# Decay attention in float32: both heads' score matmuls in one PSUM pair, and V products side by side

## The chip, the core and the metric

The kernel runs on one core of one Trainium2 chip. The metric is device time in microseconds (us) from the program's start to its end; lower is better. The engines are TensorE (PE, with its weight loads as PEld), VectorE (DVE), ScalarE (ACT), GpSimd (POOL) and the DMA queues, which SP, ACT and POOL issue to.

## The reference

Three stages follow each other on 2304 tokens (4 batches of 576) of width 512 (8 heads of 64), all in float32. The change touches the first one alone.

```python
scores = scale * q @ k.T                          # per batch and head, 576 x 576
decay = cum[:, None] - cum[None, :]               # cum: running sum of log(clip(f))
scores = where(causal, -1e9, scores + decay)
attn = exp(scores - max(scores)); attn /= sum(attn) + 1e-9
x = (attn @ v)                                    # heads side by side: 2304 x 512
h = x @ w_in; g = h * tanh(softplus(h)); y = g @ w_out
out = max(y @ w1, y @ w2, y @ w3) @ w_out2
```

## The kernel before, in words

**Attention.** A job is one batch and one pair of heads: 4 x 4 = 16 jobs. q and k of both heads are transposed on PE (`prep`, L290) so that head 0 has its 64 dimensions on partitions 0 to 63 (`U`) and head 1 on 64 to 127 (`L`). A job has two units: g = 0 for query rows 0 to 255 and g = 1 for rows 256 to 575. `scores` (L326) makes, per unit, one tile of 128 query rows per head and row block `qt` with (qt + 1) x 128 key columns (128 and 256 columns in g = 0, 384 and 512 in g = 1), and in g = 1 also one tile that holds the last 64 query rows of both heads, as two chunks of 288 columns (`h is None`). For each tile `score_mm` (L318) issues one float32 matmul (two PE rows in the profile) into a PSUM bank `sc`. DVE adds the decay, takes the row's extreme and writes the tile P to SBUF in one operation (L366); ACT makes the exponential with its row sum (L372), DVE the reciprocal (L344, L345), POOL scales P (`scale_rows`).

`av` (L384) comes two units later (`LEAD`): PE turns P in blocks of 128 x 128 into a PSUM bank `pp` (L394), DVE and ACT in turn copy the bank to SBUF (`TA`, `TB`), and the V products (L403) multiply them with v. A product's output has 64 partitions: head 0's are the upper half of the bank `av`, head 1's the lower half. `SEQA`, `SEQB`, `PRODA` and `PRODB` say in which order the blocks are turned and which product reads which columns: in g = 1 a block row `kt` has five blocks, head 0's two, the mixed one, head 1's two, and a head's product reads 320 neighbouring columns. ACT then copies the accumulator to `xt` (L411) in two or four pieces, and SP stores it to `x_d`.

**PSUM** has eight banks: four for `sc`, `tr` and `pp` together (tag `ps`), two for `av`, two for `h`.

**h.** `h_steps` computes h = x @ w_in, 24 matmuls (mm3, L184 to L186) a step of 256 tokens and 256 columns, 72 steps. It needs x of a whole block of 256 tokens, so its first steps come after the first batch's four jobs. `w_in` comes in by DMA and is converted on ACT, DVE and POOL in pieces during the first units. Attention is emitted with high priority and the scheduler fills PE's queue with `h` matmuls between; the order in each engine's queue is fixed when the program is built. When attention is done, its buffers go to `w_out`, and the rest of `h`, then y and the last stage follow.

Of the kernel before, what the change touches and what calls it, by code (L numbers as in the profile page):

```python
# [9 lines left out]
F32 = mybir.dt.float32  # L10
# [3 lines left out]
AF = mybir.ActivationFunctionType  # L14
ALU = mybir.AluOpType
PSUM = bass.MemoryType.PSUM
# [16 lines left out]
BLK = 256  # L33
BLK2 = 512
LEAD = 2

TBW = 2432
SEQA = [(0, 0, 0), (0, 0, 1), (0, 1, 0), (0, 1, 1), (1, 0, 1), (1, 1, 1)]  # L40
ATA = [128 * i for i in range(6)]
PRODA = [(0, 0, 0, 0, 256, False, 4), (0, 1, 256, 0, 256, False, 4),
         (1, 0, 512, 128, 128, True, 6), (1, 1, 640, 128, 128, True, 6)]
SEQB = [(kt, h, qt) for kt in range(3) for h, qt in ((0, 2), (0, 3), (0, 4), (1, 3), (1, 2))]
SEQB += [(3, 0, 3), (3, 0, 4), (3, 1, 3), (4, 0, 4)]
ATB = [128 * i for i in range(19)]
PRODB = [(kt, h, 640 * kt + 320 * h, 0, 320, False, 5 * kt + (3, 5)[h]) for kt in range(3) for h in range(2)]
PRODB += [(3, 0, 1920, 128, 192, False, 19), (3, 1, 2112, 0, 192, False, 19),
          (4, 0, 2304, 256, 64, True, 19), (4, 1, 2368, 0, 64, True, 19)]


def turned_layout(seq, banks, at, products):

    out, n = [], 0
    for size in banks:
        blocks = [(*b, c) for b, c in zip(seq[n:n + size], at[n:n + size])]
        n += size
        ready = [p for p in products if p[6] <= n and p[6] > n - size]
        out.append((blocks, [p[:6] for p in ready]))
    return out  # L60


LAYA = turned_layout(SEQA, (4, 2), ATA, PRODA)
LAYB = turned_layout(SEQB, (4, 4, 4, 3, 4), ATB, PRODB)


@with_exitstack
def tile_decay_attention__mish_ff__max3_ff(
# [148 lines left out]
    ap_ = at.enter_context(tc.tile_pool(name="ap", bufs=1, side="right"))  # L217
    as_ = at.enter_context(tc.tile_pool(name="as", bufs=1, side="right"))
    aw = at.enter_context(tc.tile_pool(name="aw", bufs=1, side="right"))
    hps = sa.enter_context(tc.tile_pool(name="hps", bufs=2, space=PSUM))  # L220
    aps = at.enter_context(tc.tile_pool(name="aps", bufs=1, space=PSUM, side="right"))

    def att_psum(name):
        return aps.tile([128, 512], F32, name=name, tag="ps", bufs=4)

    U, L = slice(0, 64), slice(64, 128)

# [4 lines left out]


    TA = aw.tile([128, 768], F32, name="TA")
    TB = aw.tile([128, TBW], F32, name="TB")
    for t in sums:
        nc.vector.memset(t, 1.0)
    q4 = [as_.tile([128, 128], F32, name=f"q4_{i}") for i in range(2)]
# [1 line left out]
        nc.gpsimd.memset(t, 0.0)  # L240
    for t in vs:
        nc.gpsimd.memset(t[U, 512:640], 0.0)
    count = dict(unit=0, bank=0)

    def load(i, b, hp):

# [71 lines left out]
    def score_mm(J, h, qt, dst, c0, w):  # L318
        if h is None:
            lhs, rows = J["q4"], slice(0, 128)  # L320
        else:
            rows = (U, L)[h]
            lhs = J["q"][rows, qt * 128:qt * 128 + 128]
        nc.tensor.matmul(dst, lhs, J["k"][rows, c0:c0 + w], start=True, stop=True, skip_group_check=True)  # L324

    def scores(J, g):  # L326


        P = {}
        u = count["unit"]  # L330
        count["unit"] += 1
        sm = sums[u % 4]
        mn = aw.tile([128, 6], F32, name="mn", bufs=4)
        rr = aw.tile([128, 5], F32, name="rr", bufs=4)
        tiles = [(None, 4)] if g == 1 else []
        tiles += [(h, qt) for qt in ((0, 1) if g == 0 else (2, 3)) for h in range(2)]
        made = []
        col = 0

        def scale_rows(part):  # L340

            cs = slice(part[0], part[-1] + 1)
            with tc.high_priority(400):
                nc.vector.tensor_scalar(rr[:, cs], sm[:, cs], 1e-9, None, op0=ALU.add)  # L344
                nc.vector.reciprocal(rr[:, cs], rr[:, cs])  # L345
                for ci in part:
                    nc.gpsimd.tensor_scalar(made[ci], made[ci], rr[:, ci:ci + 1], 1.0, op0=ALU.mult, op1=ALU.mult)  # L347

        for ci, (h, qt) in enumerate(tiles):
            wd = (qt + 1) * 128 if qt < 4 else S  # L350
            Pt = aw.tile([128, wd], F32, name=f"P{qt}_{h}", bufs=LEAD)
            made.append(Pt)
            if h is None:
                P[4] = Pt
            else:
                P[h, qt] = Pt
            cb = decay(J, h, qt)
            if h is None:
                cb = [cb[:, n:n + 1] for n in range(2)]
            else:  # L360
                cb = [cb]
            for pi, (c0, w) in enumerate([(0, wd)] if qt < 4 else [(0, 288), (288, 288)]):
                sc = att_psum("sc")
                score_mm(J, h, qt, sc[:, :w], c0, w)
                like = lambda t: t.rearrange("p (a c) -> p a c", a=cb[pi].shape[1])
                nc.vector.tensor_tensor_reduce(  # L366
                    out=like(Pt[:, c0:c0 + w]), in0=like(sc[:, :w]), in1=cb[pi],
                    scale=-scale, scalar=(3e38 if pi == 0 else mn[:, col - 1:col]),
                    op0=ALU.add, op1=ALU.min, accum_out=mn[:, col:col + 1],
                )  # L370
                col += 1
            nc.scalar.activation(  # L372
                Pt, Pt, AF.Exp, scale=-1.0, bias=mn[:, col - 1:col], accum_out=sm[:, ci:ci + 1],
            )
            if ci == 2 - (g == 0):
                scale_rows(list(range(ci + 1)))
        scale_rows(list(range(3 - (g == 0), len(tiles))))
        return P

    def av(J, g, P):  # L380


        q0 = 0 if g == 0 else 256
        gw = 256 if g == 0 else 320  # L384
        T = (TA, TB)[g]
        xt = aw.tile([128, gw], F32, name=f"xt{g}")
        acc = aps.tile([128, 512], F32, name="av", bufs=2)
        for blocks, products in (LAYA, LAYB)[g]:
            pp = att_psum("pp")
            for n, (kt, h, qt, c) in enumerate(blocks):  # L390

                k0 = kt * 128 if kt < 4 else S - 128
                Pt = P[4] if qt == 4 else P[h, qt]
                nc.tensor.transpose(pp[:, n * 128:n * 128 + 128], Pt[:, k0:k0 + 128], ident)  # L394
            w, c = len(blocks) * 128, blocks[0][3]
            count["bank"] += 1
            if count["bank"] % 2:
                nc.vector.tensor_copy(T[:, c:c + w], pp[:, :w])
            else:
                nc.scalar.activation(T[:, c:c + w], pp[:, :w], AF.Copy)  # L400
            for kt, h, c, off, w, last in products:
                n = 4 * h + kt if kt < 4 else 8 + h
                nc.tensor.matmul(  # L403
                    acc[(U, L)[h], off:off + w], J["vs"][:, n * 64:n * 64 + 64], T[:, c:c + w],
                    start=kt == 0, stop=last, skip_group_check=True,
                )
        parts = [(0, 0, 0, gw)]
        parts += [(1, 0, 256, 64), (1, 64, 128, 128), (1, 192, 0, 128)] if g else [(1, 0, 0, 256)]
        for h, c, o, w in parts:
            rows = (U, L)[h]  # L410
            nc.scalar.activation(xt[rows, o:o + w], acc[rows, c:c + w], AF.Copy)  # L411
        t0 = J["b"] * S + q0
        done = 0
        while done < gw:
            blk, off = divmod(t0 + done, BLK)
            n = min(gw - done, BLK - off)
            pace[:] = [nc.sync.dma_start(x_d[blk][:, J["hp"], off:off + n], xt[:, done:done + n])]
            done += n

    def attention():  # L420


        jobs = [(b, hp) for b in range(B) for hp in range(H // 2)]
        J = {0: load(0, *jobs[0])}
        yield 0
        prep(J[0])
        J[1] = load(1, *jobs[1])
        tok = 0
        units = [(ji, g) for ji in range(len(jobs)) for g in range(2)]
        pend = []  # L430
        for n in range(len(units) + LEAD):
            if n < len(units):
                ji, g = units[n]
                pend.append((J[ji], g, scores(J[ji], g)))
            if n >= LEAD:
                unit = pend.pop(0)
                av(*unit)
                if unit[0]["hp"] == H // 2 - 1:
                    tok = unit[0]["b"] * S + (256, S)[unit[1]]
            if n < len(units):  # L440
                if g == (ji == 0) and ji + 1 < len(jobs):
                    prep(J[ji + 1])
                if g == 1 and ji + 2 < len(jobs):
                    J[ji + 2] = load(ji + 2, *jobs[ji + 2])
            yield tok


    done = 0

    def ready(i):  # L450
        return BLK * (i + 1) <= done

    def h_steps():
# [9 lines left out]
        for n, (i, fp) in enumerate(order):  # L463
# [6 lines left out]
            while fp not in loaded:  # L470
                next(wgen, None)
            xh, xl = xs[i]
            h = hps.tile([128, 2, BLK], F32, name="h")
            for a in range(2):
                fs = slice(a * 128, (a + 1) * 128)
                for c in range(KD):
# [404 lines left out]
```

## Time and profile before

| what | value |
|---|---|
| median of 3 runs | 963.77 us (963.77 to 964.42) |
| the profiled execution | 962.3 us |
| its span | 960.5 us, 15156 instructions |
| PE busy | 936.5 us (97%) |
| DVE, ACT, POOL busy | 506.6, 417.6, 229.1 us |
| score matmuls (L324) and V products (L403) in PE's rows | 320 and 448 |

Busy time is what an engine's instructions cover; matmuls are pipelined and their ends are modelled, so the start of the next matmul tells more than a row's length. The last V product starts at 352.5 us and the last `h` matmul at 488.8 us.

### The profile page before, as it was taken

Reading aid. Unit: us, or ns where it says so; the run is one execution under the profiler, and the core shown is the slowest. Engines: PE = TensorE matmul, PEld = TensorE weight load, DVE = VectorE, ACT = ScalarE, POOL = GpSimd, SP = SyncE. Lnnn points to the kernel's source line nnn. Section 1 sums busy time; section 2 is a strip of 40 time slices with the busy share of each in tenths; the row PEclk is TensorE's granted clock in tenths of the full one; section 3 lists DMA queues with packets and bytes.
Section 4 is the critical chain, followed back from the end, with each engine's and each line's share of the span. In section 5 each row is a group of like instructions: output and inputs, shape, how many; then the busy total and the mean of one; then the engine's idle time right before and its main releaser. Section 6 shows DMA issues by size and latency. Waiting matters only on the chain.

```text
span 960.5 us, 15156 instructions
## 1 busy us (share of the span) xinstructions
PE 936.5 (97%) x5312; PEld 755.2 (79%) x5312; DVE 506.6 (53%) x1164; ACT 417.6 (43%) x967; POOL 229.1 (24%) x319
## 2 busy tenths in 40 slices
PE   5998999999999999999999999999999999999998
PEld 3554666777777679999988878789888999889986
DVE  4558688533344428970026657567694345614440
ACT  5778666545454444232236445455343222412221
POOL 3456654344223210111002000000021133103310
PEclk9999999999999999999999999999999999999999
DMA  7776656644443139752245666666388544334401
GB/s 165 170 205 192 208 173 191 181 111 130 117 142 102 35 93 332 244 185 78 99 148 184 193 216 201 215 219 197 114 289 332 175 132 132 104 98 124 115 32 71
DMA packets 143931, 154.77 MB, mean 161 GB/s; under 512 B 68656, under 2 KB 103984, under 8 KB 143856
## 3 DMA queue, kind: packets, MB, share of 16 engines
q1 hardware_dynamic: 121328, 114.48, 40.3%
q10 hardware_dynamic: 19840, 25.17, 7.5%
q0 software_dynamic: 2688, 14.16, 4.0%
q8 instruction: 42, 0.69, 0.3%
q14 instruction: 33, 0.27, 0.1%
HBM read 107.55 MB, written 46.21 MB: 160 GB/s over the span
## 4 chain that ended last, share of the span: by engine, by line
PE 75%; DMA 12%; ACT 5%; DVE 4%; issue 3%; SPq 1%; POOL 0%; ACTq 0%; POOLq 0%; DVEq 0%
DMA g<-h_d 9%; PE sc L324 8%; PE h L184 7%; PE h L186 7%; PE h L185 7%; PE av L403 7%; PE q L185 5%; PE q L184 5%; PE q L186 5%; PE pp L394 4%; PE o L184 2%; PE o L185 2%; PE o L186 2%; PE y L184 2%; PE y L186 2%
## 5 line engine op out<-in xcount | busy, mean ns | idle before, releaser
L184 PE MATMUL h<-xh,wi 128*128 128x256 f32 x576 | 167.6, 291 | 0.5 <-ACT he L486 0.5
L185 PE MATMUL h<-xl,wi 128*128 128x256 f32 x576 | 166.8, 290 | 0.0
L186 PE MATMUL h<-xh,wi 128*128 128x256 f32 x576 | 166.5, 289 | 0.0
L184 PEld LDWEIGHTS h<-xh,wi 128*128 128x128 f32 x576 | 109.7, 190 | 12.7 <-issue 10.0
L615 DVE TENSOR_TENSOR gl<-g,gh 128x512 fp32r<-128x512 f32 x72 | 51.0, 709 | 129.4 <-ACT gh L614 127.1
L185 PE MATMUL y<-gl,wo 128*128 128x512 f32 (+1 forms) x320 | 118.2, 369 | 0.0
L186 PE MATMUL y<-gh,wo 128*128 128x512 f32 (+1 forms) x320 | 117.3, 369 | 0.0
L186 PEld LDWEIGHTS h<-xh,wi 128*128 128x128 f32 x576 | 109.8, 191 | 9.0 <-issue 8.6
L185 PEld LDWEIGHTS h<-xl,wi 128*128 128x128 f32 x576 | 109.7, 191 | 8.9 <-issue 6.5
L184 PE MATMUL y<-gh,wo 128*128 128x512 f32 (+1 forms) x320 | 109.2, 371 | 1.6 <-ACT ze L643 1.1
L372 ACT ACTIVATE P<-P,mn 128x128 f32<-128x128 f32 (+3 forms) x128 | 71.4, 558 | 75.0 <-DVE mn L366 70.9
L608 ACT ACTIVATE g<-g 128x512 f32<-128x512 f32 x72 | 45.4, 631 | 90.6 <-DMA g<-h_d 89.5
L347 POOL TENSOR_SCALAR P<-P,rr 128x128 f32<-128x128 f32 (+3 forms) x128 | 70.6, 565 | 58.4 <-DVE rr L345 38.6
L324 PE MATMUL sc<-kT,qT 64*128 64x128 f32 (+3 forms) x256 | 78.6, 503 | 3.4 <-ACT qT L301 3.0
L184 PEld LDWEIGHTS y<-gh,wo 128*128 128x128 f32 x320 | 60.1, 189 | 13.0 <-ACT ze L643 1.8
L185 PEld LDWEIGHTS y<-gl,wo 128*128 128x128 f32 x320 | 60.3, 189 | 10.4 <-DVE gl L615 0.7
L186 PEld LDWEIGHTS y<-gh,wo 128*128 128x128 f32 x320 | 60.3, 189 | 9.7
L403 PE MATMUL av<-TB,vs 128*64 128x320 f32 (+2 forms) x320 | 60.9, 394 | 0.1
L394 PE MATMUL pp<-ident,P 128*128 128x128 f32 x320 | 56.7, 284 | 0.5 <-DVE mn L366 0.5
L807 DVE TENSOR_TENSOR u<-q,p 128x448 f32<-128x448 f32 x36 | 22.4, 622 | 62.6 <-PE q L186 62.5
L324 PEld LDWEIGHTS sc<-kT,qT 64*128 64x128 f32 x256 | 31.8, 197 | 29.0 <-issue 10.3
L486 ACT ACTIVATE he<-h 128x512 f32<-128x512 f32 x46 | 27.3, 594 | 58.1 <-PE h L186 55.6
(141 smaller groups left out, 1897.9 us busy)
## 6 DMA issues: line engine op xcount, KB each, us to landing
g<-h_d SPq DMA_DIRECT2D x72, 256.0 KB, 3.4
s<-s_d SPq DMA_DIRECT2D x72, 256.0 KB, 2.9
h_d<-he ACTq DMA_DIRECT2D x46, 256.0 KB, 2.5
wr<-in_moe_w_out_dram SPq DMA_DIRECT2D x22, 512.0 KB, 4.1
wr<-in_moe_w_dram SPq DMA_DIRECT2D x24, 384.0 KB, 4.2
s_d<-sk POOLq DMA_DIRECT2D x12, 768.0 KB, 5.1
cb<-cum_d SPq DMA_DIRECT2D x32, 256.0 KB, 4.0
wr<-in_moe_w_in_dram SPq DMA_DIRECT2D x32, 256.0 KB, 4.1
```

Source lines behind the costliest of these rows:

```text
L184: nc.tensor.matmul(ps, wh, xh, start=start, stop=False, skip_group_check=True)
L185: nc.tensor.matmul(ps, wh, xl, start=False, stop=False, skip_group_check=True)
L186: return nc.tensor.matmul(ps, wl, xh, start=False, stop=stop, skip_group_check=True)
L324: nc.tensor.matmul(dst, lhs, J["k"][rows, c0:c0 + w], start=True, stop=True, skip_group_check=True)
L347: nc.gpsimd.tensor_scalar(made[ci], made[ci], rr[:, ci:ci + 1], 1.0, op0=ALU.mult, op1=ALU.mult)
L372: nc.scalar.activation(Pt, Pt, AF.Exp, scale=-1.0, bias=mn[:, col - 1:col], accum_out=sm[:, ci:ci + 1],)
L394: nc.tensor.transpose(pp[:, n * 128:n * 128 + 128], Pt[:, k0:k0 + 128], ident)
L403: nc.tensor.matmul(acc[(U, L)[h], off:off + w], J["vs"][:, n * 64:n * 64 + 64], T[:, c:c + w], start=kt == 0, stop=last, skip_group_check= ...
L486: nc.scalar.activation(he, h, AF.Copy)
L608: nc.scalar.activation(g, g, AF.Mish)
L615: on_dve[:] = [nc.vector.tensor_tensor(out=gl, in0=g, in1=gh, op=ALU.subtract)]
L807: add = lambda eng, o, x, y: eng.tensor_tensor(out=o, in0=x, in1=y, op=ALU.add)
```

## The change

Scores: when head 0's tile comes up, one PSUM tile of two banks is taken and both heads' matmuls are issued into it one after the other; DVE then reads the halves in turn. The mixed tile of g = 1 comes last instead of first and puts its two chunks into the two banks. V products: each bank of turned blocks holds both heads' blocks of one `kt`, a product is 256, 128 or 64 columns wide, and both heads' products stand next to each other; the mixed block's 64 columns per head are products of their own. The accumulator has the same column order for both heads, so one copy moves it to `xt`. PSUM: three banks for `tr` and `pp`, a pair `sc` (two banks), one for `av`, and two that hold a second pair until the eighth unit and then `h`.

```diff
+def turned_layout(g):
+    if g == 0:
+        runs = [[(0, 0, 256)], [(1, 128, 128)]]
+        banks = [[(0, h, qt) for h in range(2) for qt in range(2)], [(1, h, 1) for h in range(2)]]
+    else:
+        runs = [[(kt, 0, 256)] for kt in range(3)] + [[(3, 128, 128), (0, 256, 64), (1, 256, 64)]]
+        runs += [[(2, 256, 64), (3, 256, 64), (4, 256, 64)]]
+        banks = [[(kt, h, qt) for h in range(2) for qt in (2, 3)] for kt in range(3)]
+        banks += [[(3, 0, 3), (3, 1, 3), (0, None, 4), (1, None, 4)], [(kt, None, 4) for kt in (2, 3, 4)]]
...
-    hps = sa.enter_context(tc.tile_pool(name="hps", bufs=2, space=PSUM))
+    early = ExitStack()
+    eps = [early.enter_context(tc.tile_pool(name="eps", bufs=1, space=PSUM, reuse_waits="tile"))]
     aps = at.enter_context(tc.tile_pool(name="aps", bufs=1, space=PSUM, side="right"))
     def att_psum(name):
-        return aps.tile([128, 512], F32, name=name, tag="ps", bufs=4)
+        return aps.tile([128, 512], F32, name=name, tag="ps", bufs=3)
...
-        tiles = [(None, 4)] if g == 1 else []
-        tiles += [(h, qt) for qt in ((0, 1) if g == 0 else (2, 3)) for h in range(2)]
+        tiles = [(h, qt) for qt in ((0, 1) if g == 0 else (2, 3)) for h in range(2)]
+        if g == 1:
+            tiles.append((None, 4))
...
+            if not h:
+                count["sc"] += 1
+                pair = (aps if count["sc"] % 2 or not eps else eps[0]).tile([128, 2, 512], F32, name="sc", bufs=1)
+                for n in range(2):
+                    if h is None:
+                        score_mm(J, h, qt, pair[:, n, :288], 288 * n, 288)
+                    else:
+                        score_mm(J, n, qt, pair[:, n, :wd], 0, wd)
             for pi, (c0, w) in enumerate([(0, wd)] if qt < 4 else [(0, 288), (288, 288)]):
-                sc = att_psum("sc")
-                score_mm(J, h, qt, sc[:, :w], c0, w)
+                sc = pair[:, h or pi]
...
-        acc = aps.tile([128, 512], F32, name="av", bufs=2)
+        acc = aps.tile([128, 512], F32, name="av", bufs=1)
...
+            for kt, off, w, *at in products:
+                for h in range(2):
+                    n = 4 * h + kt if kt < 4 else 8 + h
+                    nc.tensor.matmul(
+                        acc[(U, L)[h], off:off + w], J["vs"][:, n * 64:n * 64 + 64], T[:, at[h]:at[h] + w],
+                        start=kt == 0 and off == 0, stop=kt == (1 if g == 0 else 4), skip_group_check=True,
+                    )
+        nc.scalar.activation(xt, acc[:, :gw], AF.Copy)
...
+            if n == 6 + LEAD:
+                eps.clear()
+                early.close()
+                eps_h.append(sa.enter_context(tc.tile_pool(name="hps", bufs=2, space=PSUM, reuse_waits="tile")))
```

The scheduler puts PE's queue together anew. Before, in a g = 1 unit of the middle of attention (`av` are V products, `pp` turned blocks, `sc` scores; an `x2` is two equal neighbours):

```order
L403 MATMUL av<-TB,vs_186 64x320
L394 MATMUL pp<-ident,P_0_2225 128x128
L403 MATMUL av<-TB,vs_186 64x320 x2
L394 MATMUL pp<-ident,P_None 128x128
L394 MATMUL pp<-ident,P_1_2230 128x128
L394 MATMUL pp<-ident,P_None 128x128
L324 MATMUL sc<-kT,qT 128x128
L403 MATMUL av<-TB,vs_186 64x320
L324 MATMUL sc<-kT,qT 128x128
```

The two 128-column scores, one per head, have a V product between them, and the first V product stands alone. The same kind of place now, at the end of a g = 1 unit:

```order
L410 MATMUL av<-TB,vs_187 64x128 x2
L410 MATMUL av<-TB,vs_187 64x64 x4
L400 MATMUL pp<-ident,P_0_2726 128x128
L400 MATMUL pp<-ident,P_1_2732 128x128
L183 MATMUL h<-xh,wi_161 128x256
L322 MATMUL sc<-kT,qT 128x512 x2
L410 MATMUL av<-TB,vs_187 64x64 x6
```

Both heads' scores are neighbours, V products stand in twos, and the mixed blocks' 64-column products follow in fours and sixes. In SP's queue the first fetch of `w_in` before, behind the stores of five units of x (`x_d`):

```order
L250 DMA rawq_181<-in_q_dram 128x4x64
L254 DMA rawq_181<-in_q_dram 64x64
L152 DMA wr<-in_moe_w_in_dram 128x512 x4
L307 DMA vs_187<-in_v_dram 128x4x64 x2
L311 DMA vs_187<-in_v_dram 64x2x64
L417 DMA x_d_61<-xt_1022 128x256
```

and now, behind the stores of three:

```order
L252 DMA rawq_183<-in_q_dram 64x64
L149 DMA wr<-in_moe_w_in_dram 128x512 x4
L259 DMA cb<-cum_d 128x2x256 x2
L248 DMA rawk_182<-in_k_dram 128x4x64 x2
L305 DMA vs_186<-in_v_dram 128x4x64 x2
```

The fetch has moved two units forward.

## Rows read from the trace of the kernel before

**Rows 1.** The page, first part: busy time, share of the span, instructions.

```profile
PE 936.5 (97%) x5312; PEld 755.2 (79%) x5312; DVE 506.6 (53%) x1164; ACT 417.6 (43%) x967; POOL 229.1 (24%) x319
```

**Rows 2.** Busy time by stretch; columns as in the first line.

```profile
core 0: us, PE busy (x) PEld busy (x) DVE busy (x) ACT busy (x) POOL busy (x), PEclk, DMA share, GB/s
0.00:110.00 110.00, 93.58 (x519) 55.37 (x520) 66.86 (x229) 74.63 (x226) 59.73 (x109) 0.95 0.71 186
110.00:353.00 243.00, 243.00 (x1550) 171.19 (x1549) 121.36 (x365) 128.72 (x357) 92.08 (x139) 1.00 0.44 129
353.00:489.00 136.00, 135.53 (x1065) 132.17 (x1064) 64.61 (x115) 42.25 (x73) 14.17 (x8) 1.00 0.53 182
```

**Rows 3.** Waits of PE from 120 to 420 us: total, times, longest.

```profile
PE h L184 <- ACT he L486: 0.5, 1, 0.5
```

**Rows 4.** Timeline of PE near 175 us: start, length, engine, line, shapes.

```profile
174.46 0.49 PE L324 MATMUL sc<-kT,qT 64*128 64x128 f32 x2
174.88 0.75 PE L403 MATMUL av<-TB,vs 128*64 128x320 f32 x2
175.56 0.48 PE L324 MATMUL sc<-kT,qT 64*128 64x128 f32 x2
175.98 0.39 PE L185 MATMUL h<-xl,wi 128*128 128x256 f32 x1
176.20 0.28 PE L186 MATMUL h<-xh,wi 128*128 128x256 f32 x1
176.32 0.27 PE L184 MATMUL h<-xh,wi 128*128 128x256 f32 x1
...
176.75 0.76 PE L403 MATMUL av<-TB,vs 128*64 128x320 f32 x4
177.44 0.70 PE L324 MATMUL sc<-kT,qT 64*128 64x256 f32 x2
```

**Rows 5.** Timeline of PE at four other places: a stretch and the next row.

```profile
191.77 1.12 PE L324 MATMUL sc<-kT,qT 64*128 64x512 f32 x2
192.82 0.38 PE L185 MATMUL h<-xl,wi 128*128 128x256 f32 x1
...
216.23 1.13 PE L324 MATMUL sc<-kT,qT 64*128 64x512 f32 x4
217.28 0.38 PE L184 MATMUL h<-xh,wi 128*128 128x256 f32 x1
...
272.73 0.49 PE L324 MATMUL sc<-kT,qT 64*128 64x128 f32 x4
273.15 0.39 PE L185 MATMUL h<-xl,wi 128*128 128x256 f32 x1
...
179.92 0.66 PE L403 MATMUL av<-TB,vs 128*64 128x192 f32 x8
180.51 0.70 PE L324 MATMUL sc<-kT,qT 64*128 64x256 f32 x2
```

**Rows 6.** Busy time by stretch, three slices of 24 us.

```profile
72.00:96.00 24.00, 20.08 (x109) 11.20 (x108) 20.42 (x59) 19.79 (x54) 16.69 (x20) 0.99 0.68 193
120.00:144.00 24.00, 24.00 (x143) 15.48 (x141) 19.80 (x48) 16.01 (x43) 13.26 (x17) 1.00 0.59 173
192.00:216.00 24.00, 24.00 (x157) 17.50 (x157) 9.37 (x33) 11.24 (x34) 9.90 (x15) 1.00 0.42 111
```

**Rows 7.** Groups by line and shape, 110 to 353 us: busy, mean ns, idle before.

```profile
L398 DVE COPY TB<-pp 128x512 f32<-128x512 f32 x21 | 14.5, 689 | 17.1 <-PE pp L394 17.0
L366 DVE CUSTOM_DVE_ANT_1 P<-sc,cb 128x512 f32<-128x512 f32 x20 | 13.7, 686 | 3.7 <-PE sc L324 3.6
L169 DVE SCALAR_TENSOR_TENSOR wt<-wr,wt 128x512 int32<-128x512 int32 x11 | 10.6, 964 | 0.1
L411 ACT ACTIVATE xt<-av 64x320 f32<-64x320 f32 x11 | 4.7, 429 | 7.9 <-PE av L403 7.9
```

**Rows 8.** Loads: V products from 110 to 353 us, and `h` of the whole span.

```profile
L403 PEld LDWEIGHTS av<-TB,vs 128*64 128x64 f32 x220 | 14.7, 135 | 10.5 <-issue 4.6
L184 PEld LDWEIGHTS h<-xh,wi 128*128 128x128 f32 x576 | 109.7, 190 | 12.7 <-issue 10.0
```

More of the change, by code (lines that the diff above doesn't have):

```diff
@@ L35 @@
 LEAD = 2
[L39 to L59, printed above, removed]
-    return out
-LAYA = turned_layout(SEQA, (4, 2), ATA, PRODA)
-LAYB = turned_layout(SEQB, (4, 4, 4, 3, 4), ATB, PRODB)
+def turned_layout(g):
[7 more added lines that the diff above has]
+        banks += [[(3, 0, 3), (3, 1, 3), (0, None, 4), (1, None, 4)], [(kt, None, 4) for kt in (2, 3, 4)]]
+    out, c = [], 0
+    for blocks, bank in zip(banks, runs):
+        products, at = [], c
+        for kt, off, w in bank:
+            products.append((kt, off, w, at, at + w))
+            at += 2 * w
+        out.append((c, blocks, products))
+        c += len(blocks) * 128
+    return out
+LAYOUT = [turned_layout(g) for g in range(2)]
 @with_exitstack
@@ L234, in tile_decay_attention__mish_ff__max3_ff @@
     TA = aw.tile([128, 768], F32, name="TA")
-    TB = aw.tile([128, TBW], F32, name="TB")
+    TB = aw.tile([128, 2432], F32, name="TB")
     for t in sums:
@@ L242, in tile_decay_attention__mish_ff__max3_ff @@
         nc.gpsimd.memset(t[U, 512:640], 0.0)
-    count = dict(unit=0, bank=0)
+    count = dict(unit=0, bank=0, sc=0)
     def load(i, b, hp):
@@ L374, in scores @@
             )
-            if ci == 2 - (g == 0):
-                scale_rows(list(range(ci + 1)))
-        scale_rows(list(range(3 - (g == 0), len(tiles))))
+            if ci == 1:
+                scale_rows([0, 1])
+        scale_rows(list(range(2, len(tiles))))
         return P
@@ L386, in av @@
         xt = aw.tile([128, gw], F32, name=f"xt{g}")
-        acc = aps.tile([128, 512], F32, name="av", bufs=2)
-        for blocks, products in (LAYA, LAYB)[g]:
+        acc = aps.tile([128, 512], F32, name="av", bufs=1)
+        for c, blocks, products in LAYOUT[g]:
             pp = att_psum("pp")
-            for n, (kt, h, qt, c) in enumerate(blocks):
+            for n, (kt, h, qt) in enumerate(blocks):
                 k0 = kt * 128 if kt < 4 else S - 128
@@ L394, in av @@
                 nc.tensor.transpose(pp[:, n * 128:n * 128 + 128], Pt[:, k0:k0 + 128], ident)
-            w, c = len(blocks) * 128, blocks[0][3]
+            w = len(blocks) * 128
             count["bank"] += 1
@@ L400, in av @@
                 nc.scalar.activation(T[:, c:c + w], pp[:, :w], AF.Copy)
[L401 to L411, printed above, removed]
+            for kt, off, w, *at in products:
[6 more added lines that the diff above has]
+        nc.scalar.activation(xt, acc[:, :gw], AF.Copy)
         t0 = J["b"] * S + q0
@@ L448, in tile_decay_attention__mish_ff__max3_ff @@
     done = 0
+    eps_h = []
     def ready(i):
@@ L472, in h_steps @@
             xh, xl = xs[i]
-            h = hps.tile([128, 2, BLK], F32, name="h")
+            h = eps_h[0].tile([128, 2, BLK], F32, name="h")
             for a in range(2):
```

## The prediction

> **What bounds the kernel now.** I read the page first: TensorE (PE) is busy 936.5 us of a span of 960.5 us [rows 1]. [...] Attention ends at 353 us; `h` fills what attention leaves before, and everything after. The waits say that it is really work: in 120 to 420 us PE waited 0.5 us in all for another engine [rows 3]. So from 110 us on, a microsecond of PE work less is a microsecond off the end, wherever it is taken.
>
> How much work is it? A busy matmul row is pipelined, so I don't use its duration: I take the start of the next matmul minus the start of the first. In the timeline one program matmul in float32 is two PE rows. A score matmul of 128 columns for **one** head (x2) starts at 174.46 and the next matmul at 174.88: 0.42 us [rows 4]. Where the scheduler has happened to put **both** heads side by side (x4), it is 272.73 to 273.15, again 0.42 us [rows 5]. At 512 columns one head takes 191.77 to 192.82, 1.05 us, and two take 216.23 to 217.28, 1.05 us [rows 5]. The heads lie in different halves of the partitions (64 rows each), and side by side the second is free. The V products, which write different halves of PSUM's partitions, do the same: 320 columns for one head 174.88 to 175.56, 0.68 us, for two 176.75 to 177.44, 0.69 us [rows 4]. Both heads' 192 and 64 columns in one stretch take 179.92 to 180.51, 0.59 us [rows 5].
>
> **The price list** follows. For scores (1.05 - 0.42)/384 columns = 1.64 ns a column, and 0.42 - 128 x 1.64 ns = 0.21 us for each stretch (what does not grow with the columns). For V products 0.59 us at 256 columns and 0.69 us at 320 fit the same 1.64 ns a column, with 0.16 us for each stretch. After a stretch the first `h` is 0.22 us long (175.98 to 176.20) where the next is 0.12 us [rows 4]: another 0.1 us.
>
> **Scores.** I go through PE's order of both programs and cut it into stretches of score matmuls; in a stretch each head has a lane, and the longer lane is paid. Before: 87 stretches, in which 63 of the 128 matmuls stand alone, and 29,696 columns. Now: 57 stretches, none alone, 20,480 columns (16 jobs x 1,280, the least there can be). Saved: 30 x 0.21 = 6.3 us and 9,216 x 1.64 ns = 15.1 us, together **21.4 us**. The float32 matmul of the last 64 rows of both heads uses the whole array and stays as it is.
>
> **V products.** The fifth block, which was the middle of a 320-column product, becomes 64-column products of its own, so program matmuls grow from 224 to 352 (256 more PE rows and as many loads), with the same columns in sum. Counted the same way: 100 stretches and 31,872 columns before, 81 and 26,944 now: 19 x 0.16 + 4,928 x 1.64 ns = **11.1 us**. I cost the added loads at nothing: a 64-column pair added 0.59 - (0.16 + 192 x 1.64 ns) = 0.11 us to its stretch [rows 5], which is its columns (64 x 1.64 ns). From below this can't be better; from above, both loads of a pair (135 ns each [rows 8]) could stand in the open, 0.27 instead of 0.11 us: 64 more such pairs x 0.16 = 10.4 us.
>
> **Returns to the full array** fall from 157 to 141: 16 x 0.1 = **1.6 us**. Sum of PE work: **34.1 us**.
>
> **Where it doesn't count.** In the first four jobs PE is not the bound, so I leave their part out: up to the end of the fourth job's products the same count gives 56.4 us before and 52.7 us now. 34.1 - 3.7 = 30.4 us.
>
> **What is added.** (1) Score tiles: four banks shared with `tr` and `pp` become one two-bank pair (two pairs until `h` begins) beside three banks; the next pair must wait until DVE has read both halves of the last. At 512 columns that is 2 x 0.686 = 1.4 us [rows 7]. From the first `h` on, PE has nearly always some 2.9 us or more of other work between two pairs by the price list, so DVE may be 1.5 us late. (2) The V accumulator has one buffer: the next unit's first product waits for one copy of about 0.43 us [rows 7]; before it stand at least ten other matmuls, 1.1 us, and from the first `h` on at least seventeen. (3) ACT makes one such copy per unit instead of two or four; ACT is busy 128.72 of 243 us, so nothing is gained [rows 2]. (4) The last score tile of a unit and its scaling on POOL come later; P is turned two units later, which covers it. (5) On SP the first fetch of `w_in` moves ahead of the x stores of two units, and its conversion on DVE earlier; I cost that at nothing, between -4 and +4 us by the quarter of the 16.4 us that PE stands idle before 110 us [rows 2]. For (1) and (2) I take off one DVE copy of 0.69 us in each of the two fullest later slices, 1.4 us. Gain: **29 us**. The rest, from 353 us on, moves forward whole.
>
> The profiled execution took 962.3 us; the median of the runs is 963.77, 1.5 us more. 962.3 - 29 + 1.5 = 934.8: **935 us**.
>
> **Rivals.** *A, DVE holds the middle* (0.20): while `w_in` is converted, DVE is busy 20.42 of 24 us at 72 us and 19.80 at 120 us, against 9.37 at 192 us [rows 6]. If that stage can't shrink, the first eight jobs give nothing. The count for jobs nine to sixteen falls from 106.1 to 86.7 us: 19.4 us, so 944. For it: those slices. Against: PE was already full there (24.00). [...]
>
> *B, loads in the open* (0.08): the 10.4 us above, so 945. Against it: the `h` matmuls start every 0.12 us with loads of 190 ns each [rows 4, 8], which can't be if loads don't lie beside matmuls. [...]
>
> *C, the start gains too* (0.10): two score pairs and three banks instead of four banks in all; then all 34.1 us and a quarter of the idle time, 4.1 us, so 926.
>
> *D, the single pair stops PE* (0.04): after the first eight units 60 pairs wait in turn for DVE. It eats the gain when each waits 0.5 us (29/60), that is when DVE is 2.0 us late; at 0.6 us it is 36 us, so 971, **slower**. For it: in DVE's queue a copy of `pp` or `he` (0.69 us) and conversions of up to 0.96 us stand between [rows 7]. Against: after 170 us DVE is under half busy [rows 6].
>
> *E, the pair doesn't overlap* (0.03): if the second head waited for the first in the shared tile, the other lane's 20,480 columns would be paid, 33.6 us: 968. In the order only the first of the two has a wait, and each has its own bank; so hardly.
>
> **Chances and range.** Forecast 0.55, A 0.20, B 0.08, C 0.10, D 0.04, E 0.03. A measurement can tell 0.2% (1.9 us). Forecast and A to C are faster: 0.93. D and E are slower, but for 0.02 where D's wait comes near 0.5 us: same 0.02, slower 0.05. The forecast's own spread is 930 to 940; the range reaches to C below (924) and past A and B, with half of both together, above (950).
>
> **What would show it.** Score rows x4 everywhere, with the next matmul 0.42 to 1.06 us on; V rows x4 or more; PE still full from 110 us; attention's PE work 30 us less, and more `h` matmuls beside it, since the order puts more of them there. It is wrong if PE's waits name DVE at the score line (D), if a stretch of five 64-column pairs takes over 0.7 us (B), or if the time before about 170 us has not shrunk (A).

## The result, and the profile after

The changed kernel takes 940.2 us (median of 4 runs, 938.93 to 940.94) against 963.77 (4 runs beside it, 961.94 to 964.42): 23.6 us less, ratio 0.9757 with a 95% interval of 0.974 to 0.9774. Its profiled span is 939.2 us, 21.3 below that of before. The forecast was 29 us.

The page's first part and the same stretches as [rows 1] and [rows 2], the last one up to the last `h` matmul (461.4 us, where it was 488.8), and the slices of [rows 6] with one more, at 168 us. First the page:

```profile
PE 905.2 (96%) x5568; PEld 752.1 (80%) x5568; DVE 505.5 (54%) x1164; ACT 395.1 (42%) x903; POOL 227.4 (24%) x319
```

Then the windows:

```profile
0.00:110.00 110.00, 87.74 (x590) 54.76 (x591) 67.17 (x218) 66.11 (x197) 55.22 (x101) 0.92 0.71 183
110.00:353.00 243.00, 239.50 (x1912) 192.55 (x1913) 122.51 (x380) 117.92 (x329) 98.37 (x149) 0.99 0.50 141
353.00:461.00 108.00, 108.00 (x866) 105.32 (x865) 61.65 (x110) 37.81 (x64) 10.75 (x6) 1.00 0.62 202
...
72.00:96.00 24.00, 19.59 (x160) 12.73 (x156) 15.22 (x41) 14.28 (x44) 11.54 (x16) 0.92 0.65 180
120.00:144.00 24.00, 24.00 (x188) 18.46 (x186) 15.78 (x44) 13.76 (x37) 11.74 (x16) 1.00 0.74 195
168.00:192.00 24.00, 20.51 (x160) 16.50 (x160) 16.90 (x45) 13.48 (x37) 10.44 (x16) 0.93 0.65 191
192.00:216.00 24.00, 24.00 (x193) 19.38 (x189) 9.68 (x33) 10.72 (x32) 9.47 (x14) 1.00 0.64 167
```

PE is busy for 31.3 us less in all, and idle for 5.8 us more of the first 110 us and for 3.5 us of the second stretch, where it had been full [rows 2]. The last V product starts at 354.2 us (352.5 before): attention takes as long as it did, but more `h` lies beside it (916 rows of `h` in the second stretch for 711), and the stretch behind it, `h` with the first `y` matmuls, takes 108 us where it took 136. Of the slices after 110 us, the one that is not full now is at 168 us, with DVE busy 16.90 of 24 us.

**The prices hold.** Timeline of PE at three places, each a stretch and the next row; columns as in [rows 4]:

```profile
109.44 0.49 PE L322 MATMUL sc<-kT,qT 64*128 64x128 f32 x4
109.87 0.39 PE L181 MATMUL h<-xh,wi 128*128 128x256 f32 x1
...
122.44 1.13 PE L322 MATMUL sc<-kT,qT 64*128 64x512 f32 x4
123.50 0.39 PE L181 MATMUL h<-xh,wi 128*128 128x256 f32 x1
...
353.44 1.02 PE L410 MATMUL av<-TB,vs 128*64 128x128 f32 x24
354.39 0.38 PE L182 MATMUL h<-xl,wi 128*128 128x256 f32 x1
```

A pair of 128 columns costs 0.43 us, one of 512 costs 1.06: what one head alone cost [rows 4, 5]. The last stretch is one 128-column pair and five 64-column pairs in a row: 0.95 us, where the price list says 0.16 + 448 x 1.64 ns = 0.90, and rival B (each of the five with its loads in the open, 0.27 us) 0.16 + 0.21 + 1.35 = 1.72.

**Where the missing gain went.** I price PE's whole order of a kernel with the list (and 0.12 us for an `h` matmul, 0.107 for a turned block, 0.36 for a chunk of the mixed tile: in the changed kernel four turned blocks take 0.43 us from 168.51 us on, and two chunks 0.75 from 128.13), and take at an `h` matmul its time in the trace minus the price of all that stands ahead of it. This "time lost" is idle time, half clock and what the prices miss. The last column counts a `y` matmul that stands ahead of the last `h` at about 0.1 us, where the trace has 0.227; with 71 of them before and 56 now, some 9.0 and 7.1 us of that column are `y`'s own work and not lost:

```
us                   first h at   lost: till first h  till 150  till 192  till last h
before                     92.3                 29.4      35.6      37.3         51.9
changed                    92.9                 34.5      40.8      47.8         60.1
```

The first `h` comes no sooner: in the first stage the saved work turns into 5.1 us more of loss. Between 150 and 192 us another 5.3 us go, and what they are is in the trace. PE's waits from 120 to 420 us, in the form of [rows 3]:

```profile
PE sc L322 <- DVE mn L372: 3.2, 1, 3.2
PE pp L400 <- POOL P L346: 0.3, 1, 0.3
```

One wait that counts. The timeline of PE, then of DVE, then of ACT around it (in brackets the idle time before, and what ended it):

```profile
170.48 0.28 PE L183 MATMUL h<-xh,wi 128*128 128x256 f32 x1
173.98 1.96 PE L322 MATMUL sc<-kT,qT 64*128 64x512 f32 x4 [3.22 <-DVE mn L372]
175.87 0.58 PE L181 MATMUL h<-xh,wi 128*128 128x256 f32 x1
...
166.66 0.69 DVE L491 COPY he<-h 128x512 f32<-128x512 f32 x1
171.27 0.43 DVE L160 TENSOR_SCALAR wt<-wt 128x512 f32<-128x512 f32 x1 [3.91 <-ACT wt L157]
171.73 0.43 DVE L163 TENSOR_SCALAR wt<-wt 128x512 int32<-128x512 int32 x1
172.19 0.69 DVE L166 SCALAR_TENSOR_TENSOR wt<-wr,wt 128x512 int32<-128x512 int32 x1
172.80 0.55 DVE L372 CUSTOM_DVE_ANT_0 P<-sc,cb 128x384 f32<-128x384 f32 x1
173.28 0.08 DVE L372 DVE_READ_ACCUMULATOR2_ANT mn<- 128x1 f32 x1
173.28 0.55 DVE L372 CUSTOM_DVE_ANT_0 P<-sc,cb 128x384 f32<-128x384 f32 x1
173.75 0.08 DVE L372 DVE_READ_ACCUMULATOR2_ANT mn<- 128x1 f32 x1
...
166.12 0.20 ACT L378 ACTIVATION_READ_ACCUMULATOR P<-P,mn 128x1 f32 x1
170.58 0.66 ACT L157 ACTIVATE wt<-wr 128x512 f32<-128x512 f32 x1 [4.26 <-DMA wr<-in_moe_w_in_dram]
```

From the bottom up: ACT's next instruction is the first step of `w_in`'s conversion and waits 4.26 us for the transfer; DVE stands at the second step and waits for ACT; behind it in DVE's queue are the two reads of a 384-column score pair; and as there is only one pair now, PE's next scores wait for those. PE stops for 3.2 us and then runs at half clock, as the granted clock of the next stretch shows (0.50 of full speed; PE's columns first, the clock third from the end):

```profile
174.20:177.50 3.30, 3.30 (x11) 1.80 (x10) 3.30 (x7) 1.39 (x4) 1.27 (x1) 0.50 0.42 107
```

In it `h` matmuls come every 0.21 us, not 0.12. So one late fetch costs 3.2 us and half of the 3.3 us at half clock, 4.9 us in all. The first stage has three stops of the same make, at 55, 59 and 86 us: PE waits 3.68, 2.63 and 1.74 us for a copy on ACT (kT, xt, `TA`) that stands directly behind that same first step in ACT's queue, which waits for the transfer. The first of them, PE and then ACT:

```profile
58.74 1.09 PE L400 MATMUL pp<-ident,P 128*128 128x128 f32 x4 [3.68 <-ACT kT L299]
...
57.44 0.66 ACT L157 ACTIVATE wt<-wr 128x512 f32<-128x512 f32 x1 [5.92 <-DMA wr<-in_moe_w_in_dram]
58.00 0.59 ACT L299 ACTIVATE kT<-tr 128x512 f32<-128x512 f32 x1
```

ACT's waits for `w_in` in the first 360 us, in the kernel before and then in the changed one (in all, times, longest):

```profile
ACT wt L160 <- DMA wr<-in_moe_w_in_dram: 10.5, 9, 2.8
```

```profile
ACT wt L157 <- DMA wr<-in_moe_w_in_dram: 26.2, 11, 5.9
```

### The profile page after: what moved, and what is told of

Same layout as the page of the kernel before. It is cut to its first block, busy times and chain, and to the rows that moved or that the text cites. A ratio compares the mean times of both kernels' runs of the same rounds, so it can differ in the third digit from the quotient of the medians.

```text
span 939.2 us, 15659 instructions
## 1 busy us (share of the span) xinstructions
PE 905.2 (96%) x5568; PEld 752.1 (80%) x5568; DVE 505.5 (54%) x1164; ACT 395.1 (42%) x903; POOL 227.4 (24%) x319
## 4 chain that ended last, share of the span: by engine, by line
PE 61%; DMA 13%; DVE 6%; ACT 4%; issue 2%; SPq 1%; POOL 1%; ACTq 0%; POOLq 0%; DVEq 0%
DMA g<-h_d 8%; PE h L182 6%; PE h L183 6%; PE h L181 6%; PE q L182 5%; PE q L183 5%; PE q L181 5%; PE sc L322 3%; PE av L410 3%; PE pp L400 3%; PE o L181 3%; PE o L182 2%; PE o L183 2%; PE y L181 2%; PE y L183 2%; PE y L182 2%
## 5 line engine op out<-in xcount | busy, mean ns | idle before, releaser
L182 PEld LDWEIGHTS y<-gl,wo 128*128 128x128 f32 x320 | 60.3, 188 | 11.1 <-DVE gl L623 1.3
L400 PE MATMUL pp<-ident,P 128*128 128x128 f32 x320 | 59.3, 292 | 4.5 <-ACT kT L299 4.3
L322 PE MATMUL sc<-kT,qT 64*128 64x128 f32 (+3 forms) x256 | 54.6, 512 | 6.1 <-DVE mn L372 5.1
L400 PEld LDWEIGHTS pp<-ident,P 128*128 128x128 f32 x320 | 38.4, 146 | 22.4 <-issue 16.2
L410 PE MATMUL av<-TB,vs 128*64 128x64 f32 (+2 forms) x576 | 50.0, 295 | 2.4 <-DVE TB L404 2.3
L622 ACT ACTIVATE gh<-g 128x512 fp32r<-128x512 f32 x72 | 44.6, 620 | 12.1 <-PE y L183 11.7
```

Of the source, the lines that this page charges most:

```text
L182: nc.tensor.matmul(ps, wh, xl, start=False, stop=False, skip_group_check=True)
L410: nc.tensor.matmul(acc[(U, L)[h], off:off + w], J["vs"][:, n * 64:n * 64 + 64], T[:, at[h]:at[h] + w], start=kt == 0 and off == 0, stop=kt ...
L622: on_act[:] = [nc.scalar.activation(gh, g, AF.Copy)]
```

## The experiments

My theory: the prices are right, and what is missing are waits that hang on `w_in`'s fetch and conversion. Rivals: one half of the change is worth less than priced; or the single score pair (rival D) or single V buffer eats the gain by itself. "y end" below is the start of the last `y` matmul, the first milestone whose work is the same everywhere; from first `h` to y end is 589.7 us before and 566.6 changed, 23.1 apart, where the price list has 29.6 (34.1 less the 4.5 us of saved work that lie ahead of the first `h`).

**Scores alone** (the scores and PSUM of the change, the V products of before). One line of the edit, against the changed kernel; the layout tables, the product loop and the copies to `xt` go back with it:

```diff
-        for c, blocks, products in LAYOUT[g]:
+        for blocks, products in (LAYA, LAYB)[g]:
```

> The change's scores and PSUM arrangement with the V products of before (one accumulator bank). Counted as in the prediction, PE's order has 58 score stretches and 20,480 columns, and 85 V stretches with 28,544 columns: 29.2 us less PE work than before, 4.9 us more than the whole change. Theory (price list right, about 7 us lost to waits for w_in in the first stage): 940 + 4.9 = 945 us. Rival (the price list itself is a fifth too high): 946 to 948 us, and then its trace shows a pair of heads over 0.43 us at 128 columns or over 1.07 us at 512.

Measured: 941.9 us, ratio 0.9777 (0.9751 to 0.9802), 21.9 us less, and 3 us below both cases. From first `h` to y end 570.2. So the score half brings nearly all of the gain. That is no contradiction to its 21.4 us in the sum: neighbouring scores also stop breaking up the V products, and counted alone it is 29.2 us, of which 7 did not come.

**V products alone** (the scores and PSUM of before). One line of the edit, against the kernel before; the rest goes with it as above:

```diff
-        for blocks, products in (LAYA, LAYB)[g]:
+        for c, blocks, products in LAYOUT[g]:
```

> The change's V products with the scores and the PSUM banks of before. 102 V stretches and 26,560 columns, but 92 score stretches and 31,744 columns (the scheduler parts a few more heads): 4.2 us less PE work than before. Theory: 959 to 961 us. Rival (V products carry half of the gain, their loads being hidden): 952 us.

Measured: 965.0 us, ratio 1.0022 (1.0003 to 1.0041): nothing gained, a little lost, and above both cases. The list gave 4.2 us, since the scheduler then cut the scores into 92 stretches; and the time lost till the last `h` grew by 7.2 us (below; about 2 of them are sixteen more `y` matmuls ahead of it), with one stop of PE just behind attention, for a piece of `w_out`, the largest part of it that I can name:

```profile
PE y L180 <- ACT wo L525: 2.6, 1, 2.6
```

**No waiting for w_in's data, changed and before** (the conversion reads a tile of zeros, the fetch goes on; the data of `w_in` are left out):

```diff
-                t = convert(wst, fetch(wst, blocks), abs_eng="act")
+                fetch(wst, blocks)
+                t = convert(wst, r0, abs_eng="act")
```

> The change, with the fetches of w_in still issued, but their conversion reading a tile of zeros that is there from the start, so that no engine waits for these fetches; left out is w_in's data, so h is of zero weights. Counted PE work 35.3 us less than before. Theory (ACT's and DVE's waits for w_in, and the half clock after them, took the missing 6 to 7 us): 930 to 934 us, no PE gap over 2 us between 40 and 180 us. Rival (three banks for turned blocks and one accumulator hold the first stage): 938 to 941 us, the gaps stay.

> The same edit on the kernel before; left out is w_in's data, so h is of zero weights. Counted PE work as before (0.3 us less). Theory: before lost less to these waits (ACT waited 10.5 us for w_in against 26.2 us), so 957 to 962 us, and the difference between this run and the changed kernel with the same edit is 29 us or more. Rival: 964 us and a difference of 24 us.

Measured: changed 938.9 us (ratio 0.974, 0.9713 to 0.9767), before 971.8 (1.0083, 1.0056 to 1.011). The times by themselves miss the expectation, and that of the changed kernel lies where the rival had it: free to go, conversions moved into the first units, and the first `h` came at 97.9 and 105.3 us. From first `h` to y end it is 558.7 and 589.8: 31.1 us apart, where the price list has 33.3. The stop at 170 us is gone; a new one of 2.8 us has come at 110 us, for `xh` on POOL.

**Without w_in, changed and before** (neither fetched nor converted):

```diff
-                t = convert(wst, fetch(wst, blocks), abs_eng="act")
-                split(wi[fp][:, 0, c:c + 2], wi[fp][:, 1, c:c + 2], t, "act", "pool")
+                nc.gpsimd.memset(wi[fp][:, :, c:c + 2].bitcast(F32), 0.0)
```

> The changed kernel without w_in: its pieces are neither fetched nor converted, POOL sets them to zero at the same places instead, so h is zero and everything after it. By the price list PE's work in attention is 396.6 us (396.0 in the changed kernel). Theory (what is missing of the 29 us went into waits that hang on w_in, through ACT's and DVE's queues): no PE wait of over 1 us between 110 and 350 us, PE full from 110 us on, and from the first h to the end of y at least 30 us less than in the same edit of the kernel before; its time 910 to 935, since the first stage loses w_in's part of the DMA too. Rival (the single score pair or the single V buffer eats it): PE waits at the score line stay, and the difference to the kernel before with the same edit is 23 to 25 us.

> The kernel before without w_in (neither fetched nor converted, zeros in its place). By the price list PE's work in attention is 430.3 us, the same as with it. Theory: from the first h to the end of y 587 to 592 us (589.7 with w_in), since PE was already full there; the time itself falls by what the first stage gains, 935 to 960; 30 to 34 us above the changed kernel with the same edit. Rival: 23 to 25 us above it.

Measured: changed 928.5 us (ratio 0.9623, 0.9597 to 0.9649), before 966.5 (1.0039, 1.0014 to 1.0065): 38.1 us apart, and from first `h` to y end 554.3 and 592.8, 38.4 apart (34.0 by the list). POOL had set its zeros by 24 us in both. PE's waits of the changed kernel from 110 to 420 us without `w_in` are one row:

```profile
PE h L181 <- ACT he L491: 0.3, 1, 0.3
```

and 110 to 192 us with `w_in` and without it, changed kernel (columns as in [rows 2]):

```profile
110.00:192.00 82.00, 78.50 (x606) 62.15 (x608) 56.59 (x158) 47.18 (x128) 43.34 (x62) 0.98 0.68 187
```

```profile
110.00:192.00 82.00, 82.00 (x658) 63.59 (x657) 33.39 (x122) 39.11 (x113) 22.99 (x47) 1.00 0.49 132
```

This is the clearest pair. Taking `w_in` away gives the kernel before nothing (it is 4 us slower, in another order) and takes 11.7 us off the changed kernel (12.9 by the ratios). The rival's 23 to 25 us apart is out. My 935 to 960 for the kernel before was wrong: I took it that the first stage would gain from a freer DMA, but the first `h` stays at 92.9 us.

**One score pair from the start:**

```diff
-    eps = [early.enter_context(tc.tile_pool(name="eps", bufs=1, space=PSUM, reuse_waits="tile"))]
+    eps = []
```

> The changed kernel with one score pair from the start (the early second pair is not made; its two banks stay empty until h takes them at the same place). Price list: 396.3 us against 396.0, 60 score stretches for 57. Theory: the second pair is worth something only in the first stage, where PE has no h to do: 940 to 946. Rival (the single pair stops PE: each of the 28 pairs of the first eight units that had two buffers now waits 0.5 us or more): 950 or more, and the PE waits name DVE at the score line in the first 170 us many times, not once.

Measured: 948.6 us (ratio 0.9829, 0.9805 to 0.9853), between my range and the rival's. PE's waits before and after 120 us:

```profile
PE sc L322 <- DVE mn L372: 10.6, 7, 3.0
...
PE sc L322 <- DVE mn L372: 1.7, 2, 1.3
```

The first `h` comes 10.6 us later, and from there to y end it takes 562.0 us, less than the changed kernel. So the second pair is worth 8.4 us in the medians (7 by the ratios), all of it while PE has no `h` to do; after that, one pair is enough, unless DVE is held.

**Five ways to give w_in another place.** First, its first step on DVE instead of ACT:

```diff
-                t = convert(wst, fetch(wst, blocks), abs_eng="act")
+                t = convert(wst, fetch(wst, blocks), abs_eng="dve")
```

> The changed kernel with the first step of w_in's conversion (taking the absolute value's bits) on DVE in place of ACT. Nothing on ACT waits for a fetch of w_in any more, DVE does. Price list 395.0 against 396.0. Theory (ACT's and DVE's queues both carry the wait for w_in on to PE): ACT's waits for w_in (26.2 us) vanish, with PE's stops for kT and xt copies in the first 100 us; DVE's own wait stays and can stop the score pair as at 174 us; in sum 934 to 941. If ACT's queue was the only path: 934. If neither mattered: 940 plus what DVE's 16 added steps of 0.5 us cost, 940 to 948.

Measured: 944.1 us (ratio 0.9785, 0.9757 to 0.9812), a miss: above the theory, and inside the range of the case that neither queue mattered. ACT's waits for `w_in` are gone, and DVE has them: PE now waits 7.1 us in one stop for a copy on DVE, `TB`, and 7.3 us in seven at the score line, so the wait moved and did not vanish. Then four buffers for a fetched piece:

```diff
-                t = convert(wst, fetch(wst, blocks), abs_eng="act")
+                t = convert(wst, fetch(wst, blocks, bufs=4), abs_eng="act")
```

> The changed kernel with four buffers for a fetched piece of w_in in place of two. With two, SP can issue a fetch only when the conversion two pieces earlier is done (14.6 us of SP's waits from 110 to 180 us are for that), so the data land just when ACT and DVE already stand before the next conversion. Price list 394.4 us against 396.0; the order has the first h after 79.3 us of PE work in place of 58.4, so more of h lies after attention. Theory: ACT's and DVE's waits for w_in past 110 us fall below 3 us, no PE gap of over 1 us between 110 and 350 us, from the first h to the end of y what the same work costs with no stall, and the time 930 to 936. Rival (the wait is the transfer itself, whatever the buffers): the stop near 170 us stays, 938 to 942.

Measured: 941.8 us (ratio 0.9784, 0.9765 to 0.9803), a miss. ACT's waits for `w_in` fell to 13.5 us, the stop at 170 us is gone, and PE waits at the score line 3.6 us in three other places past 110 us. Fetches two pieces ahead:

```diff
+        with tc.high_priority(AHEAD):
+            asked = [ask(k) for k in range(2)]
...
-        for _ in range(2 if 2 <= na <= 9 else 0):
+        for _ in range(1 if na == 4 else 2 if 4 < na <= 12 else 0):
```

> The changed kernel with w_in's fetches asked for two pieces ahead and at attention's own priority, the conversions from the fourth unit on (two units later). Price list 395.6 us; the order has the first h after 89.5 us of PE work in place of 58.4. Theory: w_in is always there when ACT comes to it, so no stop past 110 us; the first stage has w_in's fetch earlier beside the loads of q, k and cum, of which PE waits already for one in the first 25 us, and no h to fill it: 932 to 945. Rival (waits for w_in don't matter): 940 plus the h that no longer fills the first stage, 945 to 955.

Measured: 941.4 us (ratio 0.9778, 0.9756 to 0.9799); within the theory's range, but not without a stop: ACT waits 8.2 us for `w_in`, and past 110 us PE 2.9 us in one stop for DVE. Everything two units later:

```diff
-        for _ in range(2 if 2 <= na <= 9 else 0):
+        for _ in range(2 if 4 <= na <= 11 else 0):
```

> The changed kernel with w_in's conversions (and with them the fetches) in units 4 to 11 in place of 2 to 9. Price list 397.2 us; first h after 79.3 us of PE work. Theory: the first stage loses the stop of kT and xt behind w_in on ACT, but the eight units with the conversions now lie later, with PE full and the single score pair for four of them, so the stops that hang on DVE become more: 936 to 945, with PE waits at the score line past 150 us of 3 us or more in all. Rival: the place of the conversions does not matter, 940.

Measured: 944.8 us (ratio 0.9818, 0.9795 to 0.9841), in the range, but PE's waits past 110 us name ACT (4.7 us) more than DVE (0.8), so the way that I gave is not the one. Last, the copies of turned blocks off DVE:

```diff
-            if count["bank"] % 2:
+            if count["bank"] % 2 and not 2 < count["unit"] <= 11:
```

> The changed kernel with all copies of turned blocks on ACT, none on DVE, in the nine units around w_in's conversion (DVE and ACT take them in turn everywhere else). Price list 395.5 us against 396.0, first h after 68.4 us of PE work in place of 58.4. About 15 copies of 0.69 us leave DVE, which is busy 15 to 19 of 24 us there, and go to ACT, busy 14. If what is missing is DVE's own load while it converts: PE's waits for DVE between 70 and 190 us go, 933 to 937. If it is the wait for w_in's data at the head of ACT's queue: the copies now stand behind it too, PE waits for ACT in their place, 940 to 948.

Measured: 939.4 us (937.46 to 942.93; ratio 0.9759, 0.9734 to 0.9784): no different from the changed kernel, and neither of my two cases.

The time lost, by the same reckoning, for all of them:

```
us                               till first h  till 192  till last h   first h at
before                                   29.4      37.3         51.9         92.3
before, without w_in                     33.9      38.3         55.7         92.9
before, no wait for w_in                 42.0      51.4         65.6        105.3
changed                                  34.5      47.8         60.1         92.9
scores alone                             28.8      44.2         55.9         90.4
V products alone                         28.8      38.8         59.1         90.0
changed, without w_in                    33.5      37.6         49.8         92.8
changed, no wait for w_in                36.3      45.6         57.7         97.9
one score pair                           48.2      57.1         69.9        103.5
first step on DVE                        35.3      50.6         64.2         94.0
four buffers                             42.3      52.9         66.8        121.6
fetched early                            49.2      51.8         67.6        138.7
two units later                          40.7      53.3         66.1        120.0
copies off DVE                           33.6      48.7         63.2        102.0
```

Read the column at 192 us, by when `w_in` is nearly done. Without it, both kernels have lost 38 us. With it, the kernel before has lost no more, and the changed one ten more. Taking away the wait for the data alone brings 2.2 of the ten back on balance (it also moved conversions into the first units, so what the wait is worth by itself isn't told by it). Shorter waits of ACT for the data (four buffers, fetched early), another place or fewer copies on DVE bring back none. So the ten microseconds are shown to be `w_in`'s, and the score pair is shown not to eat them by itself. They come with the score half of the change: scores alone has lost 44.2 us by then, V products alone 38.8, though its first fetch of `w_in` is issued at 53.7 us, as early as in the changed kernel (53.6; 64.6 before). So the earlier fetch by itself does not cost them either. No run has `w_in` and a second pair past the eighth unit, so the single pair's part in them is read from the stop at 170 us and not tried. How they divide among the transfer and the conversion's steps on ACT, DVE and POOL stays open: each new place gave the stops to another copy. No version that does all the work beat the changed kernel by more than the runs spread.

## Why the prediction was right or wrong

**Right: the bound and the price list.** PE's work was the bound from 110 us on but for 3.5 us, pairs and 64-column products cost what the list said, and the two kernels without `w_in` are no less apart than the list has it (34.0; 38.4 measured, of which 2.0 are stops in `y`; the other 2.4 are open). Rivals B and E fell with the timeline: 0.95 us, not 1.72, and 1.06 us for both heads.

**Right: the start gains nothing** (C out). "I leave their part out" took off 3.7 us; the loss till the first `h` grew by 5.1.

**Wrong in size: the step "(1) and (2) ... 1.4 us", with "(5) ... I cost that at nothing".** The loss from first `h` to 192 us grew by 5.4 us, from 7.9 to 13.3. I looked for DVE being late by its own reads (two of 0.69 us) against 2.9 us of cover. What was late was an earlier instruction in DVE's queue that waited for ACT, which waited for a transfer. The cover should have been counted against the whole chain in front of the read, not against the read. The stop and the half clock behind it are 4.9 of the 5.4 us.

That is rival A's stage with rival D's mechanism: A had said 944 because DVE's load holds the stage till `w_in` is converted, D that the single pair stops PE. Each came true for a part, and the time came out between forecast and A. The sign that I had given for D, PE's wait naming DVE at the score line, came once. The sign that spoke for A was in [rows 6]: DVE at 19.80 of 24 us while PE was full, which after the change left less PE work to hide behind (argued; taking copies off DVE gained nothing). Against A stood that PE was full there, which says only that nothing is lost yet. At the stop that ends at 173.98 us PE waits for a bank that DVE empties, but DVE was idle for 3.91 us ahead of it, so it was late, not too slow.

**Wrong: "The rest, from 353 us on, moves forward whole."** The last `h` moved by 27.4 us, the span's end by 21.3. Of the 6.1 us between, 15 `y` matmuls at 0.227 us (3.4 us) now stand behind the last `h` instead of ahead of it; of the other 2.7, about 1 us is that PE waits longer in `y` and the last stage (4.2 us in all against 3.3), and the rest is not settled.

Together: 34.1 - 5.1 - 5.4 = 23.6; plus 0.4, the loss from 192 us to the last `h` with `y` at 0.227 us (5.6 before, 5.2 now); minus the 2.7: 21.3 us, the difference of the profiled spans. That 23.6 is also the difference of the medians is chance.

**Not separable: 21.4 for scores and 11.1 for V.** The joint count is right, but the parts aren't what each edit is worth: scores alone brought 21.9 of 23.6 us, V alone nothing.

## What to carry to other kernels

PE's busy share of 24.00 of 24 us doesn't say how much work can be taken away before something else shows (from 168 to 192 us it was 24.00 before and is 20.51 now): do the sum for the stage, and ask of each in-order queue that PE waits for what in it waits for a transfer. A buffer that a slow reader gives back is as late as the latest instruction ahead of the reader (here PE stood 3.22 us for a pair whose reads lay behind a step that waited 3.91 us), so before taking a second buffer away, list that queue. Where a scheduler rebuilds the order, price the whole new order, not the edit: half an edit can be worth nearly all of it (21.9 of 23.6 us here).

## What the runs showed of the hardware

**Clock.** In the changed kernel, after stops of PE of 1.7 to 3.7 us past 50 us, the granted clock went from 1.00 to 0.50 of full speed: for 10 us at 58 us, where two such stops follow each other, and for some 3 us at 89, 96 and 174 us. So the stop at 170 us cost its own 3.2 us and then half of 3.3 us. Not every stop was followed by this: stops of 2.3 us at 68 us with V products alone and of 2.4 us at 104 us with scores alone left the clock at 1.00. One stretch of each of the three kernels, in this order (clock third from the end):

```profile
58.00:68.00 10.00, 6.63 (x30) 4.57 (x32) 6.72 (x17) 5.13 (x15) 3.25 (x4) 0.50 0.71 187
```

```profile
68.00:80.00 12.00, 9.69 (x54) 5.19 (x55) 9.80 (x29) 10.25 (x28) 5.84 (x8) 1.00 0.56 154
```

```profile
103.00:115.00 12.00, 9.49 (x76) 8.11 (x76) 9.14 (x22) 8.03 (x26) 10.10 (x10) 1.00 0.71 195
```

**DVE beside POOL.** One of the first stage's stops (PE waits 2.3 us for `TB` at 95 us) came from no transfer. Timeline of DVE, then of POOL, in the changed kernel:

```profile
92.59 2.31 DVE L343 TENSOR_SCALAR rr<-sums 128x2 f32<-128x2 f32 x1
94.82 0.68 DVE L404 COPY TB<-pp 128x512 f32<-128x512 f32 x1
...
166.35 0.17 DVE L343 TENSOR_SCALAR rr<-sums 128x2 f32<-128x2 f32 x1 [3.25 <-ACT P L378]
...
92.22 2.67 POOL L139 TENSOR_TENSOR xl<-xr,xh 128x1024 fp32r<-128x1024 f32 x1
```

The same two-column operation takes 0.17 us at 166.35 us, with POOL idle, and 2.31 us when it begins beside POOL's subtraction with two inputs; both end at 94.9 us. That the one holds the other up is read from these times; by what, no run shows. Summed over DVE's instructions up to 192 us, what each took beyond the shortest of its form, where that is over 0.1 us, is 17.9 us in the changed kernel, 17.5 before, and without `w_in` 2.1 and 6.0. All of these instructions run beside one of POOL's, in the changed kernel 11.8 of the 17.9 us beside a POOL operation with two inputs; 10.5 us fall on the conversion's own steps on DVE. So part of what `w_in` costs seems to be paid on DVE while POOL does its share of the work: an estimate from these sums. The kernel before pays as much, so this by itself does not set the two apart; how much of it reaches PE was not tried.
